# One chain of three stages on one core: wider float64-to-float32 conversion passes, one scaling of q and k, 512-column v matmuls, and a new order

## The chip, the cores and the metric

The kernel runs on one core of a Trainium2 chip. Time is device time in microseconds (us) of one launch. Below, PE is the matmul engine, PEld its weight load, DVE the vector engine, ACT the scalar engine, POOL the GpSimd engine and SP the engine that issues most transfers. Engines run their own instruction lists strictly in order, and wait for each other by semaphores.

## The reference

Inputs are q, k, v and alpha of shape (4, 8, 768, 48) in float32. Three stages follow each other; S = 768 tokens, D = 48, model width 384.

```python
# 1 attention with a decayed state, per batch and head
for t in range(S):
    state = alpha[t][:, None] * state + outer(k[t], v[t])
    y[t] = q[t] @ state
x = y.transpose(0, 2, 1, 3).reshape(4, 768, 384)
# 2 mixing over tokens, then over channels
theta = x @ w_theta
u = x + w_tok_r @ (x * cos(theta)) + w_tok_i @ (x * sin(theta))
x2 = u + relu(u @ w_ch)
# 3 gated unit with a mixing over tokens in it
h = relu(x2 @ w_in); u, v = halves(h)            # 512 columns each
v_n = (v - mean(v)) / sqrt(var(v) + 1e-6)
out = (u * (w_spatial @ v_n + b_spatial)) @ w_out
```

The weights w_theta, w_tok_r, w_tok_i, w_ch, w_in and w_out reach the core as raw float64 words. w_spatial is float32.

## The kernel before, in words

**Splitting.** A large product is made of two-part float32r operands: a part `high`, and `low` = value minus high. Three matmuls (high·high, high·low, low·high) stand for one product. So each weight is first brought from float64 to float32 and then split, on ACT and DVE, into a tile with two halves.

**Conversion (`conv`, lines 381 to 401).** Weights are cut into pieces of 128 x 384 (`CW`). A float64 piece takes a load into `raw` (`raw_f64`, issued on POOL for the first 30 pieces, on SP after), `bits` on DVE (low word shifted right by 29 into `wf`), `expo` on ACT (high word scaled into `we`), `sign` on ACT (float16 cast into the upper half of each word of `wf`), `join` on DVE (`we` shifted left, xor `wf`), `high` on ACT and `low` on DVE. There are two buffers each of `raw`, `we` and `wf`. 42 pieces are float64: 3 of w_theta, 24 of the token weights, 3 of w_ch, 8 of w_in, 4 of w_out. 12 float32 pieces of w_spatial need only `high` and `low`.

**Attention.** There are 24 units u: batch b = u // 6 and 128 tokens i = u % 6. A unit scans alpha (`att_scan`: back-to-front scan into `rt`, reciprocal, forward scan into `al`), multiplies k by `rt` into `kh` (`att_kh`, L468) and q by `al` into `qh` (`att_qh`, L475), and then runs small matmuls: `psa` (scores), `psk` (transposes of kh), `psu` (new states), `psy` (output). The states go through `ss` and `tmp` on DVE; `ss` reads `rt` (function `decay`). One half of the masked scores is moved between partitions by two small transfers (`ay<-ax`).

**Mixing.** `x` of the unit is transposed (`pst`) and split (`xh`: high on ACT, low on DVE, L596). `th` = x @ w_theta (`th_p`, 6 + 3 matmuls of 384 columns) leads through `kk`, `r`, two sines (ACT) and `z_m` to `z`, then `z_h` on ACT and `z_l` on DVE (L644) make the split tile `zs`. `tokmix` (L667) adds the unit's share of both token weights into five accumulators: 36 matmuls a unit, 18 of 512 columns and 18 of 256. After the sixth unit of a batch, `evac` adds the accumulators to x, and the channel product `psc` (`ch_h`, `ch_l`, `ch_p`, L704) runs in three parts of 256 tokens; the result goes to DRAM (`x2d`).

**Gated unit.** Per batch: v (`v_p`, L791: for each 128 tokens two groups of 9 matmuls of 256 columns), its normalisation (`v_r` to `v_l`), u (`pu`), the token mixing (`sp`), the product with u, and w_out (`po`).

**What sets the order.** All work is registered as steps with an engine, a cost, a lag, predecessors, tiles, and a priority, worked out from due times and from tables of offsets (`OFF`, `OFF0`, `OFF3`, `UNIT`, `PIECE`). `order` then plays a list schedule with these costs and emits the steps in the order in which they start there. The chip sees only that order, engine by engine. An instruction that is not ready holds up all that stand behind it on its engine.

Of the kernel before, what the change touches and what calls it, by code (L numbers as in the profile page):

```python
# [32 lines left out]
DM = H * D
# [19 lines left out]
    "raw": -579.24, "bits": 77.55, "sgn": 238.01, "mag": -986.24, "mul": -276.62, "high": -1604.02, "low": -55.01,  # L53
    "v": 65.63, "vr": 45.98, "vb": -98.38, "vw": 1530.62, "vm": -380.37, "vh": -1324.44, "vl": -603.77, "g_u": 49.47,
    "g_r": -428.27, "g_s": -238.89, "g_m": 77.82, "g_h": -145.94, "g_l": -188.62, "o_p": -179.85, "o_e": -213.43,
    "x2h": -211.54, "x2l": 369.82, "x2": -19.09,
# [193 lines left out]
def attention_mixer_kernel(  # L250
# [71 lines left out]

    def raw_f32(n):
        c = cvs[n]
        c["f"] = wst.tile([128, CW], F32, tag="cv", name="wf", bufs=CVB)
        nc.sync.dma_start(c["f"].rearrange("p (a b) -> p a b", a=c["a"]), c["src"])

    def raw_f64(n):
        c = cvs[n]
        c["raw"] = wst.tile([128, CW, 2], U32, tag="raw", name="raw", bufs=RAWB)  # L330
        c["queue"].dma_start(c["raw"].rearrange("p (a b) c -> p a (b c)", a=c["a"]), c["src"].bitcast(U32))

    def halves(x, j):
        return x.bitcast(U16).rearrange("p (c k) -> p c k", k=2)[:, :, j]

    def bits(n):
# [1 line left out]
        c["f"] = wst.tile([128, CW], F32, tag="cv", name="wf", bufs=CVB)
        if n in BITA:
            nc.scalar.activation(halves(c["f"], 0), c["raw"][:, :, 0], AF.Identity, scale=KEEP)  # L340
            return
        nc.vector.tensor_scalar(  # L342
            out=c["f"].bitcast(U32), in0=c["raw"][:, :, 0], scalar1=29, scalar2=None, op0=ALU.logical_shift_right
        )

    def expo(n):
        c = cvs[n]
        c["e"] = wst.tile([128, CW], F32, tag="ex", name="we")
        nc.scalar.activation(c["e"], c["raw"][:, :, 1].bitcast(F32), AF.Identity, scale=SHRINK)

    def sign(n):
        c = cvs[n]
        nc.scalar.copy(out=halves(c["f"], 1).bitcast(F16), in_=c["e"])  # L353
# [26 lines left out]

    def conv(src, part, key, tiles=(), scale=None):
# [5 lines left out]
        pool = scale is None and n % 4 < LOP
        c["eng"] = nc.gpsimd if pool else nc.vector
        before = [raws[-1]] if raws else []
        raw, ex, cv = ("raw", RAWB, n), ("ex", 2, n), ("cv", CVB, n)  # L390
# [761 lines left out]
```

## Time and profile before

| | |
|---|---|
| median of 3 runs | 613.5 us (613.27 to 613.8) |
| the profiled execution's own time | 614.92 us |
| its span, first to last instruction | 613.2 us |
| granted TensorE clock, mean of the span | 1.000 |
| PE busy | 580.5 us (95%), 6100 matmuls |
| DVE busy | 414.1 us (68%), 795 instructions |
| ACT busy | 269.5 us (44%), 536 instructions |
| data moved | 61.45 MB, mean 100 GB/s |

The busy time of PE is the union of its matmuls' modelled durations: a lone group of matmuls looks longer than the same group in a run. The profile cuts the span into slices: in the first three of 15.3 us each, PE is busy for 0, 5 and 8 tenths, and from the fourth on nearly always. DVE is busy for 9 tenths in slices three to five and again around 100 us, and falls to 3 to 6 tenths in the last stage.

### The profile page before, as it was taken

How to read it: one execution, taken by the hardware profiler on the slowest of the kernel's cores; microseconds unless marked ns; L12 is line 12 of the kernel's file. 1: busy time of each engine (PE TensorE's matmuls, PEld its weight loads, DVE VectorE, ACT ScalarE, POOL GpSimd, SP SyncE). 2: the span in 40 equal slices, each digit the busy share in tenths (PEclk: the TensorE clock that was granted, in tenths of full speed). 3: DMA queues.
4: the chain of work that ended last, by engine and by line, in shares of the span. 5: the costliest groups of instructions: out<-in, count | busy, mean ns of one | idle time of the engine just before them, and what ended most of it. 6: DMA issues, size and time to landing. Idle time of an engine off the chain costs nothing.

```text
span 613.2 us, 14391 instructions
## 1 busy us (share of the span) xinstructions
PE 580.5 (95%) x6100; PEld 536.8 (88%) x6100; DVE 414.1 (68%) x795; ACT 269.5 (44%) x536; POOL 31.3 (5%) x58
## 2 busy tenths in 40 slices
PE   0589998999999999999999999999999999999997
PEld 0477886887888889988889899999999999999997
DVE  5899999999779886478686686655336433553330
ACT  2567677645334343334676434623223331242122
POOL 1111111000000000000000011001000010010000
PEclk9999999999999999999999999999999999999999
DMA  8766666733533443221444454201100110001002
GB/s 230 211 206 197 188 195 176 205 104 90 154 117 96 111 123 91 79 59 58 134 127 141 138 186 168 93 11 38 40 1 1 40 40 2 0 27 52 1 0 78
DMA packets 33984, 61.45 MB, mean 100 GB/s; under 512 B 3840, under 2 KB 25472, under 8 KB 33408
## 3 DMA queue, kind: packets, MB, share of 16 engines
q1 hardware_dynamic: 31520, 48.74, 26.0%
q0 software_dynamic: 2400, 11.80, 6.5%
q8 instruction: 48, 0.79, 0.5%
q14 instruction: 16, 0.13, 0.1%
HBM read 47.94 MB, written 9.44 MB: 94 GB/s over the span
## 4 chain that ended last, share of the span: by engine, by line
PE 79%; DVE 13%; DMA 4%; issue 2%; ACT 2%; SPq 0%; DVEq 0%; ACTq 0%
PE acc L667 19%; PE sp L848 16%; PE pu L833 8%; PE po L877 8%; PE psv L791 8%; PE psc L704 6%; PE th L606 3%; PE psy L563 3%; DMA qk<-in_qka 3%; PE psu L529 2%; PE th L609 2%; DVE rt L456 1%; PE psa L489 1%; PE psk L513 1%; DVE al L460 1%
## 5 line engine op out<-in xcount | busy, mean ns | idle before, releaser
L667 PE MATMUL acc<-w,zs 128*128 128x512 f32 (+1 forms) x864 | 174.7, 347 | 0.5 <-ACT w L366 0.4
L667 PEld LDWEIGHTS acc<-w,zs 128*128 128x128 f32 x864 | 133.5, 189 | 18.9 <-ACT w L366 0.7
L848 PE MATMUL sp<-w,vns 128*128 128x384 f32 x576 | 105.8, 336 | 0.0
L848 PEld LDWEIGHTS sp<-w,vns 128*128 128x128 f32 x576 | 100.7, 188 | 0.0
L791 PE MATMUL psv<-w,xs 128*128 128x256 f32 x432 | 55.3, 282 | 0.0
L833 PE MATMUL pu<-xs,w 128*128 128x384 f32 x288 | 55.1, 334 | 0.0
L791 PEld LDWEIGHTS psv<-w,xs 128*128 128x128 f32 x432 | 54.3, 190 | 0.1
L877 PE MATMUL po<-w,gs 128*128 128x384 f32 x288 | 53.2, 335 | 0.4 <-ACT v L799 0.4
L877 PEld LDWEIGHTS po<-w,gs 128*128 128x128 f32 x288 | 49.8, 188 | 0.7 <-ACT v L799 0.7
L833 PEld LDWEIGHTS pu<-xs,w 128*128 128x128 f32 x288 | 50.2, 188 | 0.0
L864 ACT CAST gs<-t 128x384 fp32r<-128x384 f32 x32 | 16.4, 513 | 70.1 <-DVE t L858 70.1
L857 DVE TENSOR_TENSOR t<-sp,bsb 128x384 f32<-128x384 f32 x32 | 17.8, 556 | 42.7 <-PE sp L848 42.0
L704 PE MATMUL psc<-us,wch 128*128 128x256 f32 x324 | 42.7, 284 | 0.6 <-DVE us L692 0.6
L704 PEld LDWEIGHTS psc<-us,wch 128*128 128x128 f32 x324 | 40.6, 191 | 1.1 <-DVE us L692 0.8
L606 PE MATMUL th<-wth,xh 128*128 128x384 f32 x144 | 32.2, 361 | 4.8 <-DVE xh L596 3.7
L811 POOL TENSOR_TENSOR rs<-rs,mhalf 128x1 f32<-128x1 f32 x24 | 14.8, 619 | 407.5 <-PE psc L704 219.1
L353 ACT CAST wf<-we 128x384 f16<-128x384 f32 x42 | 26.4, 629 | 17.2 <-DVE wf L342 16.7
L489 PE MATMUL psa<-qh,kh 48*64 48x64 f32 x768 | 18.1, 236 | 15.7 <-DVE qh L475 15.7
L489 PEld LDWEIGHTS psa<-qh,kh 48*64 48x64 f32 x768 | 14.7, 144 | 20.8 <-DVE qh L475 15.7
L456 DVE TENSOR_TENSOR_SCAN rt<-al,heads 112x536 f32<-112x536 f32 x24 | 30.3, 1263 | 3.0 <-DMA al<-in_qka 2.9
L606 PEld LDWEIGHTS th<-wth,xh 128*128 128x128 f32 x144 | 25.7, 199 | 6.5 <-DVE xh L596 4.5
L804 DVE BATCH_NORM_STATS2 stt<-v 128x6 f32<-128x512 f32 x24 | 16.5, 689 | 21.9 <-ACT v L799 21.7
(79 smaller groups left out, 899.9 us busy)
## 6 DMA issues: line engine op xcount, KB each, us to landing
qk<-in_qka SPq DMA_DIRECT2D x24, 448.0 KB, 4.5
al<-in_qka SPq DMA_DIRECT2D x24, 234.5 KB, 2.9
vd<-in_vt SPq DMA_DIRECT2D x24, 192.0 KB, 3.6
raw<-in_w_tr POOLq DMA_DIRECT2D x12, 384.0 KB, 3.8
raw<-in_w_ti POOLq DMA_DIRECT2D x12, 384.0 KB, 3.9
x2d<-xT SPq DMA_DIRECT2D x12, 384.0 KB, 3.1
x<-x2d SPq DMA_DIRECT2D x4, 1152.0 KB, 5.1
out<-o SPq DMA_DIRECT2D x24, 192.0 KB, 1.9
```

Source lines behind the costliest of these rows:

```text
L353: nc.scalar.copy(out=halves(c["f"], 1).bitcast(F16), in_=c["e"])
L456: nc.vector.tensor_tensor_scan(out=back[:, ::-1], data0=line[:, ::-1], data1=one[:, ::-1], initial=1.0, op0=ALU.mult, op1=ALU.add)
L489: nc.tensor.matmul(st[u]["psa", e][o0:o0 + 64, h, c, :], kh[r0:r0 + D, a, c, :], qh[r0:r0 + D, a, c, :], start=True, stop=True,)
L563: nc.tensor.matmul(psy[par][64 * c:64 * c + 64, a, :], w, v, start=part == 0 or first, stop=part == 1,)
L606: nc.tensor.matmul(th, xh[:, 0, k], wth[:, pr, k], start=(k == 0 and pr == 0), stop=False)
L667: nc.tensor.matmul(acc[b, n][:, c0:c1], zs[:, pl, ri, m * 128:(m + 1) * 128], w[:, pr, t0:t1], start=first and n != 1, stop=last, skip_gro ...
L704: nc.tensor.matmul(ps, wch[:, pl, k, m * 128:(m + 1) * 128], us[:, pr, k], start=(n == 0), stop=(n == 3 * KD - 1),)
L791: nc.tensor.matmul(ps[:, c], xs2[:, pl, k, o:o + 128], w[:, pr, k], start=(n == 0), stop=(n == 3 * KD - 1),)
L833: nc.tensor.matmul(pu, win[f // 2][:, pl, (f % 2) * KD + k], xq[b, h][:, pr, k], start=(n == 0), stop=(n == 3 * KD - 1),)
L848: nc.tensor.matmul(sp[:, :TH], vns[b, s][:, pl, f * 128:(f + 1) * 128], wsp[s][:, pr, h], start=(n == 0), stop=(n == 3 * NS - 1),)
L857: nc.vector.tensor_tensor(out=t1, in0=s2.pop(("sp", b, f, h))[:, :TH], in1=bsb[0][:, t], op=ALU.add)
L877: nc.tensor.matmul(po, gs[b][:, pl, f, s * 128:(s + 1) * 128], wo[f // 2][:, pr, f % 2], start=(n == 0), stop=(n == 3 * KF - 1),)
```

## The change

- A float64 piece is now up to 768 wide (`CW` = S), so that 42 pieces become 22: 12 for the token weights, 2 each for w_theta and w_ch (768 and 384 wide), 4 for w_in, 2 for w_out. w_spatial goes in 6 pieces.
- The raw words are loaded two bytes further on, so that one 32-bit view of the buffer holds the middle of each float64 and another, 16-bit, view its top. `top` (ACT) writes the top half as float16, scaled by 0.5, into the upper halves of one zeroed buffer `zeros`. `join` (DVE) shifts the middle word right by 13 and ors it with `zeros`. The result is 256 times too small, and `high` and `low` multiply by 256. `bits`, `expo`, `sign` are gone. There are two `raw` buffers, one `zeros` and one `wf`. POOL clears `zeros` once at the start.
- k and q are scaled in place by one instruction (`att_qk`) over 1024 columns, with the scan results `al` and `rt` now two halves of one tile. There are 2 such tiles (before: 3 of `al`, 2 of `rt`), and 3 buffers of `qk` (before: 2, and separate `kh` and `qh`).
- The channel product of batches 0 to 2 runs in two parts of 384 tokens; batch 3 keeps three of 256. `v_p` is one group of 9 matmuls of 512 columns.
- `bsb` is loaded later (in `open_b`), and two instead of three v tiles stand in the first pool (`VNA`).
- The planner has a shared "wire" for transfers, other lags, and new tables; so nearly all lists are in a new order.

```diff
-    "al": -660.59, "qk": 104.21, "vn": -248.52, "vt": -161.42, "sc": 151.44, "kh": 164.6, "q": 513.27, "A": -285.97,
+    "al": -1577.34, "qk": 547.82, "vn": -222.7, "vt": 980.4, "sc": 1168.33, "kh": 913.04, "q": 424.2, "A": -293.18,
...
+XLP = ()
+NQ = 16
+QKB = 3
+ALB = 2
+CHN = 2
+VNA = 2
...
-                    if shared:
+                    if e in ("dma", "queue"):
+                        wire = max(wire, now + cost) + shared
+                    elif shared:
                         cost += max(now, port) - now
                         port = now + cost
...
-    CW = 384
+    CW = S
...
+    zeros = wst.tile([128, CW], U32, tag="zeros", name="zeros", bufs=1)
+    nc.gpsimd.memset(zeros, 0)
...
+        a, b = c["src"].shape[1:]
+        w = 4 * a * b
+        r = wst.tile([128, 4 * CW + 4], U16, tag="raw", name="raw", bufs=RAWB)
+        c["top"], c["rest"] = r[:, 4:w + 4].bitcast(BF16), r[:, 2:w + 2].bitcast(U32)
+        c["queue"].dma_start(r[:, 1:w + 1].rearrange("p (a b) -> p a b", a=a), c["src"].bitcast(U16))
+
+    def top(n):
...
+        out = zeros[:, :a * b].bitcast(F16).rearrange("p (c k) -> p c k", k=2)[:, :, 1]
+        nc.scalar.activation(out, c["top"].rearrange("p (c k) -> p c k", k=4)[:, :, 0], AF.Identity, scale=0.5)
 
     def join(n):
...
-            out=fb, in0=c["e"].bitcast(U32), scalar=3, in1=fb, op0=ALU.logical_shift_left, op1=ALU.bitwise_xor
+            out=f.bitcast(U32), in0=c["rest"].rearrange("p (c k) -> p c k", k=2)[:, :, 0], scalar=13,
+            in1=zeros[:, :a * b], op0=ALU.logical_shift_right, op1=ALU.bitwise_or,
         )
...
     def load_al(u):
-        st[u]["al"] = pa.tile([112, 8, SEG], F32, tag="al", name="al", bufs=3)
+        t = pa.tile([112, 2 * 8 * SEG + 4], F32, tag="al", name="al", bufs=ALB)
+        st[u]["al"], st[u]["rt"] = (t[:, n:n + 8 * SEG].rearrange("p (g j) -> p g j", g=8) for n in (0, 8 * SEG))
...
+    def att_qk(u):
+        x = st[u]["qk"].rearrange("p (c g j) -> p c g j", c=2, g=8)
+        nc.vector.tensor_tensor(out=x, in0=x, in1=st[u]["ar"], op=ALU.mult)
...
-        ps = psc[b, h, m] = ps_tile([128, 256], "psc")
+        ps = psc[b, h, m] = ps_tile([128, S // ch_n(b)], "psc")
...
-        ps = s2["ps", b, s] = ps_tile([128, 2, 2, 128], "psv")
...
+        ps = s2["ps", b, s] = ps_tile([128, DH], "psv")
+        n = 0
+        for k in range(KD):
+            for pl, pr in ((0, 0), (0, 1), (1, 0)):
+                nc.tensor.matmul(
+                    ps, xs2[:, pl, k, o:o + 128], win[pr, "v"][:, k],
+                    start=(n == 0), stop=(n == 3 * KD - 1),
+                )
```

What the new order does is shown at two places. The first is the start of DVE's list, from the first scan on. Before, it reads as follows (`rt` and `al` are scan results, `raw` to `wf` to `wth` the conversion of w_theta, `kh` and `qh` the first unit's scaled k and q):

```order
L456 SCALAR_TENSOR_TENSOR rt<-al,heads 112x536
L459 RECIPROCAL al<-rt 112x8
L460 SCALAR_TENSOR_TENSOR al<-al,heads 112x536
L342 TENSOR_SCALAR wf<-raw 128x384
L456 SCALAR_TENSOR_TENSOR rt<-al,heads 112x536
L459 RECIPROCAL al<-rt 112x8
L460 SCALAR_TENSOR_TENSOR al<-al,heads 112x536
L342 TENSOR_SCALAR wf<-raw 128x384
L468 TENSOR_TENSOR kh<-qk,rt 112x512
L475 TENSOR_TENSOR qh<-qk,al 112x512
L358 SCALAR_TENSOR_TENSOR wf<-we,wf 128x384 x2
```

Now the same place on DVE reads (`qk` scaled in place is the new scaling, `w` is the first token weight):

```order
L457 SCALAR_TENSOR_TENSOR al<-al,heads 112x536
L460 RECIPROCAL al<-al 112x8
L461 SCALAR_TENSOR_TENSOR al<-al,heads 112x536
L457 SCALAR_TENSOR_TENSOR al<-al,heads 112x536
L460 RECIPROCAL al<-al 112x8
L461 SCALAR_TENSOR_TENSOR al<-al,heads 112x536
L358 SCALAR_TENSOR_TENSOR wf<-raw,zeros 128x768
L378 SCALAR_TENSOR_TENSOR w<-wf,w 128x768
L469 TENSOR_TENSOR qk<-qk,al 112x1024
L358 SCALAR_TENSOR_TENSOR wf<-raw,zeros 128x768
L469 TENSOR_TENSOR qk<-qk,al 112x1024
L491 TENSOR_TENSOR ax<-psa,cst_sb 128x256
```

The first unit's scaling stood behind two short shifts of w_theta; it now stands behind the whole join and low part of a 768-wide piece of w_tok_i.

On POOL, the weight loads before begin with w_theta in three pieces:

```order
L331 DMA raw<-in_w_theta 128x768 x3
L331 DMA raw<-in_w_tr 128x768 x2
L331 DMA raw<-in_w_ti 128x768 x2
L331 DMA raw<-in_w_tr 128x768 x2
L331 DMA raw<-in_w_ti 128x768 x2
```

Now POOL clears `zeros`, and then loads:

```order
L331 MEMSET zeros 128x768
L346 DMA raw<-in_w_ti 128x3072
L346 DMA raw<-in_w_theta 128x2x1536
L346 DMA raw<-in_w_tr 128x3072
L346 DMA raw<-in_w_theta 128x1536
L346 DMA raw<-in_w_ti 128x3072
```

A token piece now comes ahead of the first part of w_theta, and another ahead of its last part.

The second place is later on DVE, at the end of the first batch's states (`ss` and `tmp` of units 4 and 5, and the scan of unit 6):

```order
L532 TENSOR_TENSOR ss<-tmp,al 112x192
L378 SCALAR_TENSOR_TENSOR w<-wf,w 128x768
L540 TENSOR_TENSOR tmp<-psu,ss 112x192
L358 SCALAR_TENSOR_TENSOR wf<-raw,zeros 128x768
L620 SCALAR_TENSOR_TENSOR r<-kk,th 128x384
L532 TENSOR_TENSOR ss<-tmp,al 112x192
L457 SCALAR_TENSOR_TENSOR al<-al,heads 112x536
```

The first `ss` here is the last reader of unit 4's `al` tile; the scan at the end needs unit 6's alpha, which is loaded into that same buffer. Five instructions stand between the two.

## Rows read from the trace of the kernel before

**Rows 1.** Windows: busy us of each engine (instructions), clock, DMA share, GB/s

```profile
0.00:16.00 16.00, 0.31 (x12) 0.32 (x16) 8.99 (x17) 3.82 (x6) 2.51 (x8) 1.00 0.86 232
16.00:45.00 29.00, 21.13 (x338) 17.04 (x330) 25.64 (x54) 17.16 (x37) 3.22 (x6) 1.00 0.70 205
45.00:130.00 85.00, 81.90 (x1222) 68.79 (x1221) 83.32 (x167) 61.09 (x129) 10.23 (x19) 1.00 0.62 180
130.00:160.00 30.00, 28.63 (x461) 24.15 (x460) 27.36 (x51) 15.97 (x36) 0.54 (x1) 1.00 0.44 128
160.00:346.00 186.00, 186.00 (x2422) 164.80 (x2421) 138.28 (x252) 84.20 (x168) 0.00 (x0) 1.00 0.36 109
346.00:600.00 254.00, 253.05 (x1613) 252.53 (x1612) 130.53 (x259) 84.91 (x159) 14.85 (x24) 1.00 0.13 44
```

**Rows 2.** Waits: longest idle of DVE between 30 and 130 us (total, times, longest)

```profile
DVE tmp L546 <- PE th L609: 0.5, 1, 0.5
```

**Rows 3.** Timeline at the start: start us, us, engine, line, operation

```profile
1.26 1.24 POOL L331 DMA_DIRECT2D raw<-in_w_theta  x2 [0.82 <-POOLq L1141]
10.30 0.55 ACT L349 ACTIVATE we<-raw 128x384 f32<-128x384 f32 x1 [1.08 <-DMA raw<-in_w_theta]
14.34 0.69 DVE L468 TENSOR_TENSOR kh<-qk,rt 112x512 f32<-112x512 f32 x1 [1.34 <-DMA qk<-in_qka]
15.69 1.14 PE L489 MATMUL psa<-qh,kh 48*64 48x64 f32 x32 [15.69 <-DVE qh L475]
20.53 0.56 DVE L377 SCALAR_TENSOR_TENSOR wth<-wf,wth 128x384 fp32r<-128x384 f32 x1 [0.59 <-ACT wth L368]
30.05 0.69 PE L606 MATMUL th<-wth,xh 128*128 128x384 f32 x1 [1.07 <-DVE xh L596]
43.80 0.95 DVE L644 TENSOR_TENSOR zs<-z,zs 128x768 fp32r<-128x768 f32 x1
44.98 1.96 PE L667 MATMUL acc<-w,zs 128*128 128x512 f32 x6
```

**Rows 4.** Chain that ended last: long matmul runs (start, us, what)

```profile
333.37 12.69 PE acc L667 x72
357.66 2.16 PE psv L791 x18
359.82 3.24 PE psc L704 x27
365.22 1.56 PE pu L833 x9
```

**Rows 5.** Timeline of DVE in the first batch, back to back

```profile
81.37 0.68 DVE L475 TENSOR_TENSOR qh<-qk,al 112x512 f32<-112x512 f32 x1
81.98 0.35 DVE L342 TENSOR_SCALAR wf<-raw 128x384 uint32<-128x384 uint32 x1
82.25 0.55 DVE L358 SCALAR_TENSOR_TENSOR wf<-we,wf 128x384 uint32<-128x384 uint32 x1
82.71 0.35 DVE L546 TENSOR_TENSOR tmp<-psu,ss 112x192 f32<-112x192 f32 x1
```

**Rows 6.** Groups by line and shape: busy us, mean ns, idle before

```profile
L353 ACT CAST wf<-we 128x384 f16<-128x384 f32 x42 | 26.4, 629 | 17.2 <-DVE wf L342 16.7
L358 DVE SCALAR_TENSOR_TENSOR wf<-we,wf 128x384 uint32<-128x384 uint32 x42 | 23.0, 551 | 3.8 <-ACT wf L353 3.6
L644 DVE TENSOR_TENSOR zs<-z,zs 128x768 fp32r<-128x768 f32 x24 | 22.8, 950 | 2.8 <-ACT zs L639 2.8
L639 ACT CAST zs<-z 128x768 fp32r<-128x768 f32 x24 | 20.1, 837 | 12.9 <-PE acc L667 6.7 <-DVE z L635 6.2
L778 DVE TENSOR_TENSOR xs<-x,xs 128x1152 fp32r<-128x1152 f32 x8 | 10.8, 1356 | 5.9 <-ACT xs L775 5.9
L676 DVE MEMSET acc<- 128x512 f32 x4 | 1.9, 485 | 0.4
```

**Rows 7.** DMA issues: KB each, median us to landing

```profile
qk<-in_qka SPq DMA_DIRECT2D x24, 448.0 KB, 4.5
al<-in_qka SPq DMA_DIRECT2D x24, 234.5 KB, 2.9
raw<-in_w_tr POOLq DMA_DIRECT2D x12, 384.0 KB, 3.8
raw<-in_w_theta POOLq DMA_DIRECT2D x3, 384.0 KB, 7.9
```

More of the change, by code (lines that the diff above doesn't have):

```diff
@@ L46 @@
 OFF = {
[6 rows of a table removed]
[L53 to L56, printed above, removed]
[6 rows of a table added]
+    "ce": 375.24, "cd": 1884.58, "raw": -103.13, "bits": 1043.49, "sgn": 478.92, "mag": -392.11, "mul": -2012.66,
+    "high": -355.36, "low": 1138.3, "v": -95.26, "vr": 388.0, "vb": 525.45, "vw": 1636.59, "vm": -1106.58,
+    "vh": -203.3, "vl": -1722.39, "g_u": -108.29, "g_r": -320.06, "g_s": -870.02, "g_m": 1030.14, "g_h": 1470.78,
+    "g_l": -450.68, "o_p": -1615.72, "o_e": -2083.69, "x2h": 181.4, "x2l": -361.14, "x2": -246.89,
 }
@@ L131, in order @@
     port = 0.0
+    wire = 0.0
     when = {}
@@ L238, in latest @@
         k = todo.pop()
-        _, _, cost, lag, after, _, _ = steps[k]
-        t = min((start[f] for f in follow[k]), default=math.inf) - SLACK * (cost + lag)
+        _, eng, cost, lag, after, _, shared = steps[k]
+        t = min((start[f] for f in follow[k]), default=math.inf) - SLACK * (cost + lag + (shared if eng in ("dma", "queue") else 0.0))
         start[k] = min(t, due.get(k, math.inf))
@@ L328, in raw_f64 @@
     def raw_f64(n):
         c = cvs[n]
[L330 to L336, printed above, removed]
-        c = cvs[n]
[L338 to L353, printed above, removed]
+        a, b = c["src"].shape[1:]
+        w = 4 * a * b
+        r = wst.tile([128, 4 * CW + 4], U16, tag="raw", name="raw", bufs=RAWB)
+        c["top"], c["rest"] = r[:, 4:w + 4].bitcast(BF16), r[:, 2:w + 2].bitcast(U32)
@@ L376, in low @@
         else:
             nc.vector.scalar_tensor_tensor(
-                out=c["part"](1), in0=f, scalar=c["scale"], in1=h, op0=ALU.mult, op1=ALU.subtract
+                out=c["part"](1), in0=c["f"], scalar=c["scale"], in1=h, op0=ALU.mult, op1=ALU.subtract
             )
@@ L384, in conv, with cost @@
         early = PIECE.get(str(n), 0.0)
-        c = {"src": src, "a": src.shape[1], "part": part, "scale": scale}
+        c = {"src": src, "part": part, "scale": scale}
         cvs.append(c)
[L387 to L390, printed above, removed]
+        size = src.shape[1] * src.shape[2] / CW
+        def cost(one, more):
+            return one + (more - one) * (2 * size - 1)
@@ L391, in conv @@
+        before = [("raw_f64", i) for i in range(2, 14)] if n >= 16 else ()
+        raw, f, zero = ("raw", RAWB, n), ("f", FB, n), ("zeros", 1, n)
         if src.dtype == I64:
             c["queue"] = nc.gpsimd if n < NQ else nc.sync
-            k0 = step(early + OFF["raw"], "queue" if n < NQ else "dma", 1.6, raw_f64, n, after=before, tiles=[raw, *tiles])
-            raws.append(k0)
-            k2 = step(early + OFF["bits"], *(("act", 0.56) if n in BITA else ("dve*", 0.27)), bits, n, after=[k0], tiles=[raw, cv])
@@ L396, in conv @@
-            k3 = step(early + OFF["sgn"], "act", 0.56, expo, n, after=[k0], tiles=[raw, ex])
-            k4 = step(early + OFF["mag"], "act", 0.43, sign, n, after=[k2, k3], tiles=[ex, cv])
-            k = step(early + OFF["mul"], "dve*", 0.47, join, n, after=[k4], tiles=[ex, cv])
-        else:
-            k = step(early + OFF["raw"], "dma", 0.8, raw_f32, n, after=before, tiles=[cv, *tiles])
-            raws.append(k)
-        k = step(early + OFF["high"], "act", 0.41, high, n, after=[k], tiles=[cv, *tiles])
@@ L403, in conv @@
-        k = step(early + OFF["low"], *(("pool*", 0.96) if pool else ("dve*", 0.47)), low, n, after=[k], tiles=[cv, *tiles])
+            k = step(early + OFF["raw"], "queue" if n < NQ else "dma", 2.6 * size, raw_f64, n, after=before, tiles=[raw])
+            k = step(early + OFF["mag"], "act", cost(0.54, 0.86), top, n, after=[k], tiles=[raw, zero])
+            k = step(early + OFF["mul"], "dve*", cost(0.47, 0.87), join, n, after=[k], tiles=[raw, zero, f])
+        else:
+            k = step(early + OFF["raw"], "dma", 1.3 * size, raw_f32, n, after=before, tiles=[raw])
+            f = raw
@@ L404, in conv @@
+        k = step(early + OFF["high"], "act", cost(0.41, 0.73), high, n, after=[k], tiles=[f, *tiles])
+        k = step(early + OFF["low"], "dve*", cost(0.47, 0.87), low, n, after=[k], tiles=[f, *tiles])
         conv_done.setdefault(key, []).append(k)
@@ L898, in attention_mixer_kernel @@
     conv_small(w_ch, wch, "wch")
-    for n, (store, name, key, pieces, a) in enumerate(w2):
-        conv_w2(store, name, key, pieces, a)
+    for one in w2:
+        conv_w2(*one)
     def ready(*key):
@@ L973, in attention_mixer_kernel @@
         k = at("zh", "act", 0.73, z_h, after=[k], tiles=[z, zs])
-        kz = at("zl", *(("pool*", 1.9) if u < ZLP else ("dve*", 0.87)), z_l, after=[k], tiles=[z, zs])
+        kz = at("zl", "dve*", 0.87, z_l, after=[k], tiles=[z, zs])
         ta = {n: (f"acc{n}", 1, b) for n in range(5)}
```

222 lines of the change are left out of this document (111 added, 111 removed), and 37 rows, old and new, of tables (OFF, OFF0, OFF3, PIECE).

## The prediction

> **What bounds the kernel now.** I read the windows first, cut where the kind of work changes. The reader is to see three regimes in the first column of busy times, PE's, beside DVE's in the third. From 160 to 600 us PE is busy for 186.00 of 186 and 253.05 of 254 us [rows 1]: there only fewer PE cycles shorten the run, and whatever DVE, ACT or a queue save is hidden behind PE. From 45 to 130 us DVE is busy for 83.32 of 85 and its longest idle is 0.5 us [rows 1, 2]. PE still reaches 81.90 of 85, so it idles 3.1 us there and 1.4 us of the 30 behind; DVE sets the pace of batch 0 by a narrow margin. In the first 45 us PE is busy for only 0.31 + 21.13 us [rows 1]. The timeline of the start, read next, says who is late: `psa` starts at 15.69 on `qh` from DVE, H0 (the first `th` matmul) at 30.05, the first token mixing at 44.98 behind `z_l` [rows 3]. [...]
>
> **PE, the sure term.** A mixing run is 72 matmuls in 12.69 us, half 512 and half 256 wide [rows 4]: 0.3525 us a pair. The old v run is 18 of 256 in 2.16 us [rows 4], 0.120 each, so one of 512 is 0.2325. Nine of these make 2.09 us where 2.16 stood; 24 such places (4 batches, 6 tiles) save 1.6 us at most, and since mixing runs overlap their loads a little differently I take 1.2. The channel product of batches 0 to 2 was 9 groups of 27 matmuls at 3.24 us [rows 4], 29.2 us. It becomes 6 groups of 27 at 384 columns; `pu` gives that width, 9 in 1.56 us [rows 4], so 0.173 each, 4.68 a group, 28.1 us. That saves 1.1. Both lie where PE is always busy, so they show in full: **2.3 us** (bounds 1.5 and 2.9).
>
> **DVE in batch 0.** In back-to-back work the start-to-start times count, since an instruction's row overlaps the next by some 0.08: `bits` takes 0.27 (81.98 to 82.25), a 384-wide join 0.46 (82.25 to 82.71), a 512-wide scaling 0.61 (81.37 to 81.98) [rows 5]. Of 768 columns `z_l` lasts 0.95, and 0.87 after the same overlap [rows 3, 6].
> - Pieces converted ahead of batch 0's end: before 3 + 24 + 3 = 30 of 384 columns; now 2 + 12 + 2 = 16, of which 14 are 768 wide.
> - `bits` goes: 30 x 0.27 = 8.1 us.
> - `join` and `low`: 60 x 0.46 = 27.6 become 28 x 0.87 + 4 x 0.46 = 26.2. Saves 1.4.
> - k and q: two of 0.61 become one of 1024 columns. No row has that width; between 768 (950 ns) and 1152 (1356 ns) [rows 6] it is 1.22 lasting, 1.14 after the overlap. Saves 0.08, 0.5 in seven units.
>
> Together about 10 us of DVE. The new join reads every second word of `raw`, which no row here does in this operation; the old join (551 ns) and `bits` (0.35 lasting) are the nearest, and between no penalty and a doubled 0.87 the cost is 0 to 12 us (14 joins); I take 0, since `bits` read the same stride and was not long [rows 5, 6].
>
> What of this shows? Only what PE can follow with: its idle time from 45 to 160 us is 3.1 + 1.4 = 4.5 us [rows 1]. Work that DVE delivers earlier ahead of 45 us would add to it. Bounds: 0 and 10. I take **5**.
>
> [...]
>
> **ACT.** A piece took 0.55 for `expo` [rows 3], 0.629 for `sign` [rows 6] and a `high`; the last two scale from 384 to 768 as casts at 629 against 837 ns [rows 6]. `top` and `high` of 768 at 0.84 to 1.26 each make 1.7 to 2.5 per 768 columns, against 2 x 1.7 = 3.4 before. ACT is busy for 61.09 of 85 us [rows 1], so its saving counts nothing; its chain counts, since `zeros` and `wf` are single: top, join, high, low of a piece cannot overlap the next piece's top and join. One cycle is about 0.9 + 0.95 + 0.84 + 0.95 = 3.6 us; twelve token pieces at that take 44 us, inside the 85 of the batch. Hidden; if DVE lags behind in the list, each break in this chain costs up to 1 us.
>
> **The start.** Before, the first theta piece was issued at 1.26 and used at 10.30, 9 us later [rows 3]. Now POOL clears 768 columns first (no row on POOL; a clearing of 512 on DVE took 485 ns [rows 6], so 0.1 to 2, I take 0.8), then loads 768 KB of `w_ti`. The two theta pieces that landed by 10.30 were also 768 KB, so `w_ti` lands near 11. Top, join, high, low then fill ACT and DVE; the first scaling stands behind that `low` in DVE's list, starts near 15 to 16 and ends 1.2 later: `psa` near 16.5 against 15.69. Theta's two parts follow on the same queue at some 9 ns per KB (384 KB in 3.8 us [rows 7]), the second only when `raw` frees: `wth` complete near 30 to 33, H0 near 33 against 30.05. Of the 3 us lost, DVE's lighter list (25.64 of 29 us busy there [rows 1], about 6 pieces without `bits` and with fewer starts, 2.5 us) gives most back before the first mixing, which I put at 45.5. Scores and states of later units, done meanwhile, make up the rest. I take **0**, bounds -3 (DVE's lighter list decides) and +10 (the loads decide).
>
> **Landing two bytes off.** No row shows it. Below: nothing. Above: twice the landing, 3.8 to 7.6 us per 384 KB; theta at the crowded start already shows 7.9 [rows 7].
> [...]
>
> **The alpha buffers.** With two, the scan of unit u+2 waits for a load that is issued only after the last `ss` of unit u. Five instructions lie between on DVE, 0.87 + 0.27 + 0.87 + 0.46 + 0.27 = 2.7 us; the load takes 2.9 after its issue [rows 7], so 0.2 us of stall, and with the issue itself, which must first see the `ss` end, I take 0.5, in five places of batch 0: 2.5 us, off the 10 DVE saves, so 7.5 remain and the 5 stands. Behind the scan its engine's list waits: conversions, `tmp`, `z_l`. With other transfers in front, up to 3 us a place.
>
> **Edits at nothing.** Later w_in, w_out and w_spatial pieces: hidden behind PE at 253.05 of 254 us; uncovered, some 3 us. `bsb` later and two v tiles: the same cover.
>
> **Sum.** 2.3 + 5 + 0 = 7.3 us. The profiled run took 614.92 (span 613.2), 1.4 above the median 613.5: 607.6 in its terms, **606.2** in the median's. A measurement here can tell about 0.2%, 1.2 us, from no change.
>
> **Rivals.**
> - *Batch 0 gives more.* The idle time of PE before 45 us shrinks too: all 10 us of DVE and 3 of the start show, 613.5 - 2.3 - 10 = 601, with bounds 597 and 603. For: DVE is the one engine without gaps [rows 2]. Against: PE has only 4.5 us to give after 45 us.
> - *The alpha loads take it back.* 5 scans stall for about 1 us beyond my estimate; with the 2.5 counted, batch 0 gains nothing and PE's term stays: 613.5 - 2.3 = 611.2 (609.5 to 613.5). For: the load cannot be issued earlier. Against: 180 GB/s leave the queues free 38% of the time [rows 1].
> - *Slower: theta lands late.* If a 768 KB piece takes two landings of 7.9 us [rows 7] instead of 9 us in all, `w_ti` lands near 17, theta's last part near 33, `wth` is done near 38 and H0 starts near 40, 10 us later. Then 613.5 - 7.3 + 10 = 616.2. It decides once H0 starts after 37.4 (30.05 + 7.3). For: the DMA share is already 0.86 in the first 16 us [rows 1]. Against: the same two landings overlap in the row at 10.30.
> - *The joins are slow* on the strided read: 12 us cancel DVE's gain, 611 to 615. I count it with the second rival.
>
> **How the numbers follow.** Forecast 0.50 (602.5 to 609.5 around 606.2), more 0.18, alpha or joins 0.17, slower 0.15. Leaving out the slower case and a sliver at the bottom gives 599 to 614. Faster by over 0.2% (below 612.3): 0.50 + 0.18 + over half of 0.17, 0.77; within it 0.08; slower 0.15.
>
> **What would show it.** Right: no `bits`; joins of 768 under 1.0 us; v runs of 9 near 2.1 us and `psc` runs of 27 near 4.7; H0 near 33, first mixing near 45; batch 0's last mixing some 5 us earlier, and the same lead kept to the end. Wrong: waits of DVE's scan on `al` over 1 us; `top` waiting for `raw` for 5 us and more late in batch 0; H0 past 37; a join near 1.5; or PE gaps after 160 us, which would say that the new order itself, and not the work, has moved the time.

## The result and the profile after

The changed kernel takes 621.84 us (median of 4 runs, 620.03 to 623.36) against 613.57 us before (613.27 to 613.80): a ratio of 1.0134, interval 1.0099 to 1.0168. It is slower by 8.3 us; the forecast was 606.2, faster, with a range up to 614. The profiled execution took 620.55 us, its span 618.4.

The windows of the kernel after (columns as in [rows 1]: time, then PE, PEld, DVE, ACT and POOL busy, granted clock, DMA share, GB/s), first in the stretches of [rows 1], then finer:

```profile
16.00:45.00 29.00, 20.09 (x344) 16.29 (x344) 23.14 (x38) 14.67 (x27) 2.66 (x5) 1.00 0.74 223
45.00:130.00 85.00, 78.16 (x1116) 65.36 (x1117) 74.15 (x118) 48.33 (x87) 4.43 (x8) 0.94 0.61 189
130.00:160.00 30.00, 30.00 (x352) 26.94 (x354) 22.19 (x36) 9.50 (x19) 0.00 (x0) 1.00 0.39 118
160.00:346.00 186.00, 185.39 (x2522) 162.11 (x2520) 138.58 (x220) 78.69 (x156) 0.00 (x0) 1.00 0.34 100
346.00:600.00 254.00, 252.33 (x1397) 240.65 (x1396) 128.71 (x246) 82.55 (x146) 15.10 (x24) 1.00 0.13 46
...
48.00:49.00 1.00, 1.00 (x4) 0.84 (x4) 0.69 (x1) 0.95 (x2) 0.00 (x0) 0.50 0.70 216
54.00:56.00 2.00, 0.41 (x2) 0.41 (x3) 2.00 (x3) 1.59 (x3) 0.00 (x0) 1.00 0.00 0
56.00:57.00 1.00, 1.00 (x10) 0.75 (x8) 1.00 (x2) 0.00 (x0) 0.00 (x0) 1.00 0.00 0
58.00:60.00 2.00, 2.00 (x32) 1.88 (x25) 2.00 (x5) 1.47 (x2) 0.53 (x1) 0.50 0.03 8
60.00:62.00 2.00, 2.00 (x11) 1.37 (x13) 1.32 (x2) 1.32 (x3) 0.29 (x1) 0.50 0.80 225
62.00:64.00 2.00, 2.00 (x36) 1.81 (x37) 0.93 (x3) 0.37 (x2) 0.23 (x1) 0.50 1.00 330
64.00:66.00 2.00, 2.00 (x27) 1.58 (x30) 1.97 (x5) 2.00 (x4) 0.00 (x0) 0.99 0.92 354
75.00:90.00 15.00, 13.39 (x202) 10.99 (x201) 13.37 (x22) 9.26 (x18) 1.54 (x3) 1.00 0.58 172
```

Most of the loss lies between 45 and 130 us. DVE did get its time back there: 74.15 us busy where 83.32 stood. But PE is busy for 78.16 us instead of 81.90, and its clock, 1.00 before, is 0.94: 0.06 x 85 = 5.1 us of full-speed work are missing, as some 10 us ran at about half the full clock (0.50 from 47 to 50 us, 0.60 from 57 to 58, 0.50 from 58 to 64). The fine windows show the pattern: PE is busy for 0.41 of 2 us (54 to 56), works for another microsecond at the full clock, and from 58 to 64 us it is busy without a gap at half its clock.

What PE waited for is read from the engines' timelines. DVE of the kernel after:

```profile
50.62 1.27 DVE L457 TENSOR_TENSOR_SCAN al<-al,heads 112x536 f32<-112x536 f32 x1 [1.93 <-DMA al<-in_qka]
53.36 0.93 DVE L638 TENSOR_TENSOR z<-z,x 128x768 f32<-128x768 f32 x1
57.08 0.55 DVE L599 TENSOR_TENSOR xh<-pst,xh 128x384 fp32r<-128x384 f32 x1
...
76.36 1.22 DVE L469 TENSOR_TENSOR qk<-qk,al 112x1024 f32<-112x1024 f32 x1 [1.69 <-DMA qk<-in_qka]
```

ACT in the same stretch:

```profile
48.44 0.51 ACT L634 ACTIVATE z<-r 128x384 f32<-128x384 f32 x1
54.32 0.83 ACT L642 CAST zs<-z 128x768 fp32r<-128x768 f32 x1 [2.36 <-DVE z L638]
55.06 0.47 ACT L581 CAST xh<-pst 128x384 fp32r<-128x384 f32 x1
```

And PE:

```profile
55.59 1.32 PE L609 MATMUL th<-wth,xh 128*128 128x384 f32 x6 [1.97 <-ACT xh L581]
...
77.68 0.58 PE L507 MATMUL psk<-cst_sb,qk 112*128 112x112 f32 x4 [1.45 <-DVE qk L469]
```

The scan of unit 4, which nobody needs yet (the scores of unit 4 start on PE at 65.71), waits 1.93 us for its alpha. Behind it in DVE's list stands `z` of unit 1, whose last sine was done at 48.95 (48.44 + 0.51); it starts at 53.36. On ACT `zs` waits for `z`, and `xh` of unit 2 stands behind `zs`. H0 of unit 2 waits for `xh`, and PE stands still. One load holds three engines through the order of their lists. At 76.36 the wait on `qk` of unit 5 holds DVE and then PE (1.45 us, until 77.68). But not every gap on PE has a slow stretch behind it: from 75 to 90 us the clock stays at 1.00.

The transfers of the alpha load in question: its issue on SP, and its landing (the only `al` load of this window):

```profile
45.38 0.33 SPq L440 DMA_DIRECT2D al<-in_qka  x1
...
DMA to landing us min/median/max: 5.2/5.2/5.2
```

It could be issued only after the last `ss` of unit 2 (at 45.01), as there are two alpha buffers, and it took 5.2 us where the median before was 2.9 [rows 7]: a 768 KB raw piece had been issued at 43.37, and `qk` followed at 46.95.

Last, the new instructions by line and shape (busy us, mean ns, idle before), against [rows 6]:

```profile
L469 DVE TENSOR_TENSOR qk<-qk,al 112x1024 f32<-112x1024 f32 x24 | 29.2, 1218 | 3.1 <-DMA qk<-in_qka 3.1
L352 ACT ACTIVATE zeros<-raw 128x768 f16<-128x768 bf16 x20 | 21.5, 1075 | 23.4 <-DMA raw<-in_w_ti 8.1 <-issue 5.0 <-DMA raw<-in_w_in 4.9
L358 DVE SCALAR_TENSOR_TENSOR wf<-raw,zeros 128x768 uint32<-128x768 uint32 x20 | 19.0, 952 | 1.9 <-ACT zeros L352 1.6
```

and the matmul runs of the critical chain (start, us, what), against [rows 4]:

```profile
223.54 4.68 PE psc L711 x27
373.14 2.10 PE psv L795 x9
```

All these came out at the forecast price.

### The profile page after: what moved, and what is told of

Same layout as the page of the kernel before. It is cut to its first block, busy times and chain, and to the rows that moved or that the text cites. A ratio compares the mean times of both kernels' runs of the same rounds, so it can differ in the third digit from the quotient of the medians.

```text
span 618.4 us, 13523 instructions
## 1 busy us (share of the span) xinstructions
PE 580.7 (94%) x5803; PEld 525.8 (85%) x5803; DVE 398.2 (64%) x671; ACT 242.1 (39%) x445; POOL 25.1 (4%) x45
## 4 chain that ended last, share of the span: by engine, by line
PE 74%; DVE 5%; DMA 3%; ACT 2%; issue 1%; POOL 0%; SPq 0%; DVEq 0%; ACTq 0%
PE acc L669 18%; PE sp L853 16%; PE pu L837 8%; PE po L882 8%; PE psv L795 7%; PE psc L711 5%; PE th L609 3%; PE psy L557 3%; PE psa L483 2%; PE psu L523 1%; DMA raw<-in_w_in 1%; PE th L612 1%; DMA x<-x2d 1%; PE psk L507 1%; PE pst L577 1%
## 5 line engine op out<-in xcount | busy, mean ns | idle before, releaser
L669 PE MATMUL acc<-w,zs 128*128 128x512 f32 (+1 forms) x864 | 178.3, 350 | 0.5 <-DVE acc L678 0.3
L795 PE MATMUL psv<-w,xs 128*128 128x512 f32 x216 | 54.3, 395 | 0.7 <-DVE xs L784 0.7
L795 PEld LDWEIGHTS psv<-w,xs 128*128 128x128 f32 x216 | 40.1, 187 | 9.0 <-DVE xs L784 1.1
L862 DVE TENSOR_TENSOR t<-sp,bsb 128x384 f32<-128x384 f32 x32 | 17.8, 557 | 45.5 <-PE sp L853 44.7
L711 PE MATMUL psc<-us,wch 128*128 128x384 f32 (+1 forms) x243 | 40.4, 319 | 0.6 <-DVE xT L721 0.6
L711 PEld LDWEIGHTS psc<-us,wch 128*128 128x128 f32 x243 | 38.0, 189 | 1.2 <-DVE xT L721 0.8
L457 DVE TENSOR_TENSOR_SCAN al<-al,heads 112x536 f32<-112x536 f32 x24 | 30.5, 1269 | 7.9 <-DMA al<-in_qka 7.8
L483 PE MATMUL psa<-qk 48*64 48x64 f32 x768 | 18.6, 236 | 17.1 <-DVE qk L469 16.1
L483 PEld LDWEIGHTS psa<-qk 48*64 48x64 f32 x768 | 15.0, 144 | 22.7 <-DVE qk L469 16.1
L352 ACT ACTIVATE zeros<-raw 128x768 f16<-128x768 bf16 (+1 forms) x22 | 22.8, 1036 | 25.5 <-DMA raw<-in_w_ti 8.1
L845 ACT ACTIVATE ur<-pu 128x384 f32<-128x384 f32 x32 | 15.7, 490 | 41.5 <-PE pu L837 24.3
```

The costliest lines, as they stand in the source:

```text
L352: nc.scalar.activation(out, c["top"].rearrange("p (c k) -> p c k", k=4)[:, :, 0], AF.Identity, scale=0.5)
L457: nc.vector.tensor_tensor_scan(out=back[:, ::-1], data0=line[:, ::-1], data1=one[:, ::-1], initial=1.0, op0=ALU.mult, op1=ALU.add)
L483: nc.tensor.matmul(st[u]["psa", e][o0:o0 + 64, h, c, :], kh[r0:r0 + D, a, c, :], qh[r0:r0 + D, a, c, :], start=True, stop=True,)
L669: nc.tensor.matmul(acc[b, n][:, c0:c1], zs[:, pl, ri, m * 128:(m + 1) * 128], w[:, pr, t0:t1], start=first and n != 1, stop=last, skip_gro ...
L711: nc.tensor.matmul(ps, wch[:, pl, k, m * 128:(m + 1) * 128], us[:, pr, k], start=(n == 0), stop=(n == 3 * KD - 1),)
L795: nc.tensor.matmul(ps, xs2[:, pl, k, o:o + 128], win[pr, "v"][:, k], start=(n == 0), stop=(n == 3 * KD - 1),)
```

## The experiments

Theory A: the arithmetic is good, and the new order, whose loads land just too late, makes PE wait, upon which the clock falls. Rivals: B, landing two bytes off is slow; C, theta's late load at the start; D, the two alpha buffers alone; E, DVE's time is not what PE waits for. In the first eight runs the changed kernel is edited, and its planner's list is kept unless said otherwise. Ratios are to executions of the kernel before that were taken with each set of runs (medians of 613.3 to 613.4 us); what a run gives back is counted from the changed kernel's 621.84 us.

**Landing on the boundary.** Rival B. (The two views of the buffer move with the load.)

```diff
-        c["queue"].dma_start(r[:, 1:w + 1]...)
+        c["queue"].dma_start(r[:, 2:w + 2]...)
```

> The raw words land on a 4-byte boundary instead of two bytes off it; the list of every engine stays. The low 19 bits of each converted weight are then wrong. Theory A (the new order lets PE wait between 53 and 58 us, and the clock falls to half behind it): landing is not the cause, pieces of 768 KB still take 5 to 7 us, time 618 to 624. Rival B (landing off the boundary is slow and holds up the conversions): pieces of 768 KB land in under 5 us, the changed kernel loses most of its 8 us, 610 to 615.

Measured: 621.03 us, 1.0125 (1.0085 to 1.0165). Issues of the kernel after (KB each, median us to landing):

```profile
raw<-in_w_ti POOLq DMA_DIRECT2D x6, 768.0 KB, 6.6
raw<-in_w_tr POOLq DMA_DIRECT2D x6, 768.0 KB, 5.3
```

and on the boundary:

```profile
raw<-in_w_ti POOLq DMA_DIRECT2D x6, 768.0 KB, 6.1
raw<-in_w_tr POOLq DMA_DIRECT2D x6, 768.0 KB, 5.9
```

One median is 0.5 us shorter and the other 0.6 us longer, and the kernel's time stays (621.03 us against 621.84). B falls.

**Three instructions moved.** Rivals A against B and C.

```diff
+        move(("z_m", 1), before=("att_scan", 4))
+        move(("att_qk", 4), after=("tr_l", 2))
+        move(("z_l", 1), after=("tr_l", 2))
```

> Three instructions of DVE's list change places: z_m of unit 1 goes ahead of the scan of unit 4, z_l of unit 1 and the scaling of unit 4 go behind tr_l of unit 2. Theory A: the two PE gaps at 53.3 to 55.6 and 57.0 to 57.7 us shrink from 3.0 to under 0.6 us and the clock stays full at 57 to 64 us, worth 2.4 + 3.4, so 615 to 617. Rival B (slow landing): the wait moves on to the next load, within 1.5 us of the changed kernel, 619 to 623. Rival C (the late start of the theta weight costs it): no change either, as H0 at 34.9 stays.

Measured: 619.44 us, 1.0091 (1.0058 to 1.0123): 2.4 us back, less than expected. Its windows:

```profile
45.00:50.00 5.00, 4.99 (x76) 4.35 (x77) 4.71 (x7) 3.63 (x6) 0.53 (x1) 0.66 0.87 276
50.00:55.00 5.00, 5.00 (x59) 4.37 (x58) 4.93 (x7) 2.25 (x6) 0.00 (x0) 1.00 0.53 176
65.00:75.00 10.00, 7.47 (x131) 6.50 (x129) 7.86 (x12) 4.79 (x9) 0.85 (x2) 1.00 0.72 208
75.00:80.00 5.00, 4.85 (x77) 3.83 (x76) 4.93 (x8) 3.61 (x8) 0.53 (x1) 0.66 0.46 134
```

The gap at 53 is closed and the clock stays full from 50 to 75. But PE, now ahead, runs into the wait on `qk` of unit 5 (2.07 us on DVE, at 73.26), idles 2.5 of 10 us, and the clock falls behind that gap instead. The time itself lies in the range that rival B gave for another reason (619 to 623); what speaks for A is the closed gap.

**More work for PE in the gaps.** What the clock costs.

```diff
+        after th_p(1, 0): its six matmuls again
+        before th_p(2, 0): tokmix(0, 0, 1) twice more
```

> More work for PE: the six H0 matmuls of unit 1 once more and six mixing matmuls of unit 0 twice more, 3.1 us at the full clock, put into the gaps at 43.3 and 53.3 us (theta of unit 1 and one accumulator of batch 0 are wrong by that). All waits stay. Theory A: the clock does not fall at 46.7 or at 57.2 us; each fall that stays out gives back 1.5 and 3.4 us, time 616 to 619 in spite of more work. If idle time alone costs and the clock is not tied to these gaps: 621 to 625.

Measured: 622.02 us, 1.0136 (1.0083 to 1.0190). The windows of the kernel after, for comparison:

```profile
45.00:50.00 5.00, 4.44 (x73) 3.87 (x74) 3.69 (x7) 2.91 (x7) 0.53 (x1) 0.70 0.85 291
55.00:60.00 5.00, 3.90 (x42) 3.39 (x43) 5.00 (x9) 2.39 (x5) 0.53 (x1) 0.72 0.01 3
60.00:65.00 5.00, 5.00 (x48) 4.04 (x47) 3.25 (x7) 2.69 (x6) 0.53 (x1) 0.60 0.91 297
```

and with the filled gaps:

```profile
45.00:50.00 5.00, 4.89 (x82) 3.87 (x82) 3.43 (x6) 3.54 (x6) 0.53 (x1) 1.00 0.94 301
55.00:60.00 5.00, 4.48 (x80) 3.64 (x80) 4.91 (x9) 2.24 (x3) 0.53 (x1) 1.00 0.15 28
60.00:65.00 5.00, 5.00 (x59) 4.24 (x58) 4.31 (x9) 3.85 (x7) 0.53 (x1) 1.00 0.97 357
75.00:80.00 5.00, 3.89 (x70) 3.07 (x72) 4.43 (x8) 2.37 (x6) 0.53 (x1) 0.73 0.35 82
```

Both falls stay out, so they followed these gaps. The gain of time that A expected did not come, and 622.02 lies in the range of the other answer: as above, PE arrives early at the wait on `qk` at 73 us, and the clock falls there (0.73). So this run does not show what a fall costs; that 3.1 us of extra matmuls cost only 0.2 us says little, as they were put where PE had been idle. A hint is that its four executions form two pairs: 619.8 and 620.0 us at a mean clock of 0.996 and 0.997, 624.1 and 625.9 us at 0.990 and 0.983. In the trace of the kernel after, the low clock came behind a wait (1.97 us, until 55.59), but not at once: right behind the gap, from 56 to 57 us, its matmuls still ran at 1.00, and from 58 us at 0.50. And PE waited for the load only through the lists of DVE and ACT.

**The loads of q and k of units 5 and 6 change places.**

```diff
+        i, j = seq.index(("load_qk", 6)), seq.index(("load_qk", 5))
+        seq[i], seq[j] = seq[j], seq[i]
```

> The loads of q and k of units 5 and 6 change places in SP's list, so that unit 5's has landed long before its scaling at 76.4 us. Theory A: the 1.7 us wait of DVE at 74.7 and PE's gap at 75.9 to 77.7 go, 1 to 2 us less, 619 to 621. Rivals B and C: no change, or the wait passes to the next load, 620 to 623.

Measured: 619.02 us, 1.0080 (1.0049 to 1.0112): 2.8 us back, somewhat more than expected. In its trace the wait on `qk` is gone, and PE is busy for 4.81 of 5 us from 75 to 80. But the scan of unit 4, which this edit does not touch, waits longer in this execution, and with it PE:

```profile
52.16 1.27 DVE L457 TENSOR_TENSOR_SCAN al<-al,heads 112x536 f32<-112x536 f32 x1 [3.51 <-DMA al<-in_qka]
```

From 45 to 130 us PE is busy for 78.06 us, no longer than in the kernel after, at a clock of 0.96. So the repair did what it was meant to do, but the profile does not show that the 2.8 us come from it alone.

**Both repairs:** the three moves and this swap together.

> Both repairs of the order at once: the three moves on DVE's list around the scan of unit 4, and the swap of the loads of q and k of units 5 and 6. Theory A (the order's waits between 45 and 80 us, and the half clock behind them, are what batch 0 lost): the two gains were 2.4 and 2.8 us alone, but the first one's kernel lost it again at the wait on q and k at 73 us, so together more than the sum, 611 to 615. If the two repair the same stretch: 617 to 619.

Measured: 617.33 us, 1.0066 (1.0048 to 1.0085): 4.5 us back, slightly less than the sum of 5.2. Theory A's number was too good; the time lies in the range for two repairs of the same stretch. Its window:

```profile
45.00:130.00 85.00, 78.75 (x1144) 65.75 (x1144) 78.47 (x121) 50.53 (x92) 4.44 (x8) 1.00 0.66 199
```

The clock is back at 1.00 in batch 0, but PE still idles 6.2 us there, in gaps of at most 1.4 us each.

**Three alpha buffers, two of q and k.** Rival D; the planner makes a new order.

```diff
-QKB = 3
-ALB = 2
+QKB = 2
+ALB = 3
```

> The buffers as they were: three of alpha, two of q and k; the planner then makes a new order for them. Rival D (two alpha buffers are the cause): scans wait no more on the alpha load, time 611 to 616. Theory A (any order has its own chance waits): another order, another time, anywhere from 610 to 628, and the waits in the trace on other tiles than alpha.

Measured: 628.71 us, 1.0247 (1.0222 to 1.0272). Waits of DVE and PE between 30 and 130 us (total, times, longest):

```profile
PE th L609 <- DVE xh L599: 4.3, 2, 3.5
...
DVE al L457 <- DMA al<-in_qka: 3.2, 2, 2.8
```

The third buffer, in an order that the tables were not made for, is no cure, and scans still wait on alpha, against what D expected. A's guess missed too: the time is above its 628, and the waits are on alpha. As the order moved with the buffers, this says nothing on the buffers alone; three buffers in the kept order were not run, so D stays open.

**Theta first.** Rival C: the first four pieces trade slots, in every step of their conversion.

```diff
-        w_ti[0], w_theta[0:2], w_tr[0], w_theta[2]
+        w_theta[0:2], w_theta[2], w_ti[0], w_tr[0]
```

> The first four pieces change places in the same slots, w_theta's two first and then the two token pieces. Rival C (theta's late part at the start costs the time): H0 starts 4 us and more before 34.9, first mixing below 45 us, time 613 to 618. Theory A: H0 is earlier but the stretch from 45 to 80 us stays, time 618 to 624.

Measured: 622.61 us, 1.0151 (1.0092 to 1.0211), within the scatter of the changed kernel. In the kernel after, H0 and ACT's `top` of a w_tr piece start as follows, and the first mixing at 46.95:

```profile
34.93 1.31 PE L609 MATMUL th<-wth,xh 128*128 128x384 f32 x3
...
39.10 1.06 ACT L352 ACTIVATE zeros<-raw 128x768 f16<-128x768 bf16 x1 [2.49 <-DMA raw<-in_w_tr]
```

With theta first:

```profile
33.08 2.27 PE L609 MATMUL th<-wth,xh 128*128 128x384 f32 x6
...
39.16 1.06 ACT L352 ACTIVATE zeros<-raw 128x768 f16<-128x768 bf16 x1 [4.01 <-DMA raw<-in_w_tr]
...
47.53 1.78 PE L669 MATMUL acc<-w,zs 128*128 128x256 f32 x7
```

H0 came 1.9 us earlier, not 4, so the trial is weaker than meant. The first mixing came no earlier at all, and the lines say why: `kk` of unit 0, the step after `th`, stands on ACT behind this `top`, which waits for its load, so `kk` starts at 40.10 here and at 40.03 in the kernel after. Again a load holds up urgent work through the order of a list. What theta alone would bring is therefore not shown; but the first mixing of the kernel after is only 2.0 us later than before [rows 3], so C falls as the main cause.

**A longer lag in the planner.**

```diff
-    LAG = {..., "dma": 1.6, "none": 0.0, "queue": 1.6}
+    LAG = {..., "dma": 2.6, "none": 0.0, "queue": 2.6}
```

> Same instructions, another order: the planner counts 2.6 us in place of 1.6 from a load's end to its use, so that uses stand further behind their loads. Theory A: waits of DVE and ACT on loads between 45 and 130 us go down, but the tables were not made for this order; 608 to 622. If loads do not matter: 618 to 626.

Measured: 628.16 us, 1.0238 (1.0215 to 1.0261), outside both ranges. The waits on loads did go down between 45 and 130 us, as A said: DVE's from 4.1 us to none. From 60 to 100 us PE is busy for 39.81 of 40, but the work around the end of batch 0 now waits, on other engines:

```profile
100.00:130.00 30.00, 27.10 (x296) 23.66 (x296) 21.27 (x34) 7.86 (x14) 0.00 (x0) 1.00 0.26 76
130.00:160.00 30.00, 25.38 (x368) 21.41 (x366) 22.51 (x35) 10.10 (x23) 0.00 (x0) 0.94 0.38 107
```

With the same kinds of instructions, three orders gave 622, 629 and 628 us. (Buffers differ in the second.)

**The new arithmetic in the old order.** The kernel before, with its own list; A against E. (A sketch of the edit; it also has three `raw` buffers where the kernel before has two.)

```diff
+            if key[0] in ("bits", "expo"):
+                continue
     sign: zeros[turn] upper halves <- top of raw, as float16, x 0.5
     join: wf <- (middle word of raw >> 13) | zeros[turn]
     high, low: x 256
```

> The kernel before in its own order, with the new arithmetic alone: pieces stay 384 wide, bits and expo are left out of the lists, top, join, high and low stand where sign, join, high and low stood, raw words two bytes off; two zeroed buffers, three of raw. Some 30 x 0.27 = 8.1 us of DVE and as many expo of ACT go out of batch 0, nothing else moves. Theory A (the arithmetic is good and the new order alone loses): PE can follow at least in part, 3 to 6 us, 607.5 to 610.5. Rival E (DVE's time in batch 0 is not what PE waits for): no gain, 612.5 to 614.5.

Measured: 609.78 us, 0.9936 (0.9918 to 0.9953). It is 3.6 us faster than the kernel before, and 12 us faster than the changed one. Its windows:

```profile
16.00:45.00 29.00, 22.70 (x379) 18.47 (x378) 26.72 (x52) 15.13 (x33) 4.40 (x9) 0.88 0.89 248
45.00:130.00 85.00, 82.84 (x1236) 70.24 (x1236) 80.78 (x151) 54.14 (x114) 9.65 (x18) 1.00 0.59 177
130.00:160.00 30.00, 29.96 (x456) 26.45 (x455) 26.39 (x47) 13.75 (x28) 0.00 (x0) 1.00 0.46 134
```

and where its first mixing starts, 3.4 us earlier than at 44.98 [rows 3]:

```profile
41.59 1.85 PE L678 MATMUL acc<-w,zs 128*128 128x512 f32 x6
```

PE gains 0.9 and 1.3 us of busy time in the two windows of batch 0 [rows 1], and the rest at the start. E's range is missed: lighter lists do reach PE, where the order lets it use them. That it is DVE's list that counts is the likely reading, as DVE had no gaps before [rows 2]; but the edit takes `expo` off ACT too, and the two were not run apart.

**v in 512 columns in the old order.**

```diff
-        ps = s2["ps", b, s] = ps_tile([128, 2, 2, 128], "psv")
-        for c in range(2): ... w[:, pr, k]
+        ps = s2["ps", b, s] = ps_tile([128, 512], "psv")
+        ... win[pr, "v"][:, k]
```

> The kernel before in its own order with v in 512 columns alone: 24 v runs go from 2.16 to 2.10 us each. By the trace after: 24 x 0.06 = 1.4 us less, 611.9 to 612.4. If the waits between the runs take it back: 613.0 to 613.6.

Measured: 612.13 us, 0.9984 (0.9972 to 0.9996): 1.3 us, near what the runs' lengths say.

**Both in the old order:** the last two edits together.

> The new arithmetic in 384-wide pieces and v in 512 columns, both in the old order. Theory A: the gains add, 4 to 8 us, 605.5 to 609.5, faster than either kernel. Rival E: only v's 1.4 us, 611.5 to 613.

Measured: 610.00 us, 0.9940 (0.9922 to 0.9958). Faster than before, but just outside A's range: v's 1.3 us do not show on top of the arithmetic. The intervals of this run and of the arithmetic alone are both about 2 us wide, so the times do not decide why. The profiles say that there was little to gain: all v matmuls together take 55.3 us in the kernel before, 53.6 with v in 512 columns, but 54.5 with the new arithmetic alone and 54.2 with both, 0.3 us less. Why v's matmuls of 256 columns are shorter beside the new arithmetic is not shown.

**Two raw buffers.** The new arithmetic in the old order, and:

```diff
-        r = wst.tile([128, w + 4], U16, tag="raw", name="raw", bufs=3)
+        r = wst.tile([128, w + 4], U16, tag="raw", name="raw", bufs=2)
```

> As e9_narrow, but with two raw buffers, so that a load waits for the join two pieces back, as in the changed kernel. If the raw buffers are what holds the conversions up: ACT's waits on raw grow, 2 us and more over e9_narrow. Theory A: within 1 us of e9_narrow.

Measured: 610.83 us, 0.9951 (0.9937 to 0.9964), 1.05 us over three buffers. That is at the edge of A's bound, and the intervals overlap; ACT's waits on `raw` are 9.8 us against 8.9. A join that holds `raw` costs little. With two raw buffers, as the kernel before has them, the arithmetic alone is worth 2.6 us.

## Why the prediction was wrong, point by point

- **What bounds the kernel: right as a reading, and incomplete.** DVE was the engine without gaps in batch 0, and a lighter list in the old order made the kernel faster (609.78 us against 613.4). What the forecast leaves out is the clock: its sum has no term for it, and the 1.00 of [rows 1] showed only that one execution of the old order had the full clock. The new list opened a gap on PE, and a slow stretch came behind it as well (clock 0.50 from 58 to 64 us).
- **PE, 2.3 us: the lengths right.** A v run is 2.10 us (forecast 2.09), a `psc` run 4.68 (4.68). v alone gave 1.3 us on the chip (1.2 forecast), and next to nothing on top of the arithmetic. `psc` was not run alone.
- **DVE in batch 0: the prices right, the step from DVE to PE wrong.** Joins at 952 ns, against 950 for `z_l` of that width [rows 6], show no charge for the strided read, the scaling is 1218 ns (forecast 1220), DVE is busy for 9.2 us less. The step that failed is "What of this shows? ... Bounds: 0 and 10. I take 5". The lower bound supposed that PE could not be served later than before. It held for the old order (2.6 to 3.6 us from the arithmetic, of the 5) and not for the new: there PE is busy 3.7 us less and lacks 5.1 us of clock.
- **The alpha buffers: the stall right, its price wrong.** I took 0.5 us in five places, 2.5 us in all; the scans of batch 0 waited 3.3 us for alpha, but in two places, and 1.93 us of it at unit 4, where the load took 5.2 us in place of 2.9 (a wait of over 1 us was among the prediction's own signs of being wrong). The error was to set the stall off against DVE's own savings, as time of DVE alone. What stands behind the scan was named only in part (not `z`), and not followed to ACT's `xh` and PE's H0, nor to the clock. The stall on `qk` of unit 5 (1.69 us) was not foreseen, nor was `top` that holds up `kk` on ACT.
- **The start: near, on the hopeful side.** H0 at 34.9 was later than the 33 forecast, first mixing 46.9 against 45.5, 2.0 us later than before where I took 0; theta loaded first brought no time. The rival that made the kernel slower through theta did not decide (H0 before 37.4).
- **Landing two bytes off: right** to count nothing for it: 621.03 us on the boundary, 621.84 off it.
- **Left out:** a rival in which the new order itself loses. "PE gaps" stood only among the signs of a wrong prediction, and only after 160 us.

The parts do not close exactly: 3.7 and 5.1 us lost from 45 to 130 us, 1.4 won in the next window, 1.0 lost from 16 to 45, 1.3 from 160 on, less 2.3 of PE's work, make 7.4, and the span grew by 5.2. PE's busy time is modelled, and a single execution scatters by as much: from 16 to 45 us, where the edit to the loads has changed nothing yet on PE, DVE or ACT, PE is busy for 20.09 us in the kernel after and for 21.59 in the run with the loads of units 5 and 6 exchanged. So the 2.2 us stay open.

**Open:** the two repairs bring back 4.5 of 8.3 us; of the other 4, the profile shows 3.1 as more idle time of PE from 45 to 130 us, in gaps of under 1.5 us. That the order alone loses is shown for the part that came back and argued for the rest: 768-wide pieces with their 768 KB loads, the single `zeros` and `wf` and two alpha buffers were never run in the old order. The price of the slow clock is not settled either: of the nine executions with both repairs, the one with the highest mean clock is the fastest (615.55 us at 1.000) and the one with the lowest the slowest (620.22 at 0.989), but the changed kernel's own do not sort so (620.03 us at 0.990, 623.12 at 0.995).

## What to carry to other kernels

An engine's list is part of its speed: here DVE was busy for 9.2 us less from 45 to 130 us and yet PE for 3.7 us less, in part because the new list put a late load (1.93 us of wait) ahead of urgent work. So follow each added wait through what stands behind it, engine by engine, to PE. Count a gap on PE together with the slow-clock stretch that may follow it: 6 us at 0.50 came here behind a wait of 1.97 us and one of 0.52, none behind that of 1.45 us at 76 us. And test new arithmetic in the old order first: it separated a gain of 2.6 to 3.6 us from a loss that hid it.

## What the runs showed of the hardware

The half clock is not as dear everywhere. In the kernel with the new arithmetic in the old order the clock is 0.88 between 16 and 45 us, about 7 us if at half (0.12 x 29 / 0.5), with PE busy for 22.70 of 29; before, PE was busy for 21.13 and the clock was 1.00. Yet its first mixing came 3.4 us earlier: at the start PE waits for others anyway. Nor is this fall peculiar to the new arithmetic: with v in 512 columns alone the clock from 16 to 45 us is 0.89. Of the 17 executions of the kernel before that were taken with these runs, five have a mean clock of 1.000 and twelve of 0.993 to 0.997, and both groups have a median of 613.4 us. So the 1.00 in [rows 1] is one execution's, and some 7 us at half the clock (an estimate from a mean clock of 0.994 over some 612 us: 0.006 x 612 / 0.5), wherever they lie in those executions, leave no mark on that kernel's time.
